# Fillers taken out of two tiles, 21 more tiny matmuls at the start, and a last half product that leaves in two parts: a sliding-window attention and ReGLU kernel on one Trainium2 core

## The chip, the core and the metric

The kernel runs on one core of one Trainium2 chip. The core has TensorE (PE in the profile; its weight loads are listed as PEld), VectorE (DVE), ScalarE (ACT), GpSimd (POOL) and SyncE (SP), each with a queue of its own that it works off in order. Engines wait for one another through semaphores. Matrix products go to PSUM, in eight banks of 128 partitions by 512 f32; everything else lies in SBUF or in HBM, and DMA engines move it.

The metric is the device time of one execution in microseconds. Before the change three runs gave 308.47, 309.38 and 309.38 us, median 309.38 us.

## What is computed

Attention over a causal window of 64 positions (8 batches, 8 heads, 576 positions, head size 64), and then a feed-forward layer whose gate is a ReLU (4608 tokens, 512 features, 1536 hidden features), all f32 outside:

```python
scores = scale * np.matmul(q, k.transpose(0, 1, 3, 2))
rel = pos[:, None] - pos[None, :]
mask = (rel >= 0) & (rel < window)              # window = 64
...
attn = attn / (np.sum(attn, axis=-1, keepdims=True) + 1e-09)
...
x = attn_out.transpose(0, 2, 1, 3).reshape(B * S, H * D)
gate = np.maximum(x @ w_gate, 0.0)
val = x @ w_val
out = (gate * val) @ w_out
```

## The kernel before, in words

The 4608 tokens are cut into nine tiles of 512 (`TT`). For a tile the kernel computes scores (`score_run`, L370 to L386: a mask product at L377 and the q k products at L385), exponentials on ACT (L645), the products with v and a column of ones (`value_block`, L388 to L392), a reciprocal and a scaling on DVE (L660, L398), a transpose on DVE (L403), the two hidden products and their gate, and the product with `w_out`.

Tile 0 takes the hidden products directly (`direct_block`, L737 on, matmuls at L750), and tiles 0 to 2 the output products too (`output`, L900 on, matmuls at L916, copy to SBUF on ACT at L927, store at L931). The other tiles use Strassen-Winograd schemes with seven half-size products in place of eight (`fast_hidden`, matmuls at L842; `fast_output`, matmuls at L1005).

The work is written in two parts. `first_part` (L408 to L509) is written out by hand: loads of the first batch, constants, a run of tiny matmuls of 32x32 by 32x16 zeros (L423 and L424, `PADS = 72` of them), scores and values of the first six windows. `second_part` (L511 to L1077) lists operations with a key, durations and dependencies, and a planner (`Plan`, L44 to L252) orders them: it plays the kernel forward with estimated durations and emits each engine's instructions in the order in which they start in that play. Nothing in it knows what the chip does; the estimates are numbers in the source.

Two things of the planner matter here.

- `fill` (L115 to L127): when the planner thinks that PE will be idle for at least 0.7 us ahead of an operation, it emits matmuls of zeros of 128x128 by 128x384 into a free bank, as many as fit at 0.165 us each with 0.25 us to spare. `emit` (L1061 to L1064) writes them. There are 21, in four groups.
- `fetch` (L93 to L113): PE's instructions come from HBM in blocks of 256. The planner assumes that block n is asked for when instruction 256 n + 165 is reached (`ASK`, L54) and must be there at instruction 256 n + 445 (`NEED`, L55). `plan.at` (L520) is the place in PE's instructions at which the second part begins, 428 + 2 PADS, since a matmul and its weight load are two instructions.

The end of the kernel is tile 8 in `fast_output`. Its last product, P4, runs in two halves `m` of six matmuls each, into columns 0 to 255 and 256 to 511 of one bank. Each half is copied by ACT (L1030) into its columns of one SBUF tile `pr`, and stored from SP (`leave`, L982 to L987). SP's queue holds the stores in order, each behind a wait for its copy and one for an earlier DMA on the same semaphore.

Of the kernel before, what the change touches and what calls it, by code (L numbers as in the profile page):

```python
# [12 lines left out]
ACT = mybir.ActivationFunctionType  # L13
# [30 lines left out]
class Plan:  # L44
# [33 lines left out]
    def op(self, name, key, engines, fn, after=(), take=(), give=(), dma=None):  # L78
        after = [a for a in dict.fromkeys(after) if a is not None]
        o = Op(name, key, engines, fn, after, take, give, dma)  # L80
        self.n += 1
        o.n = self.n
        self.all.append(o)
        for a in after:
            a.feeds.append(o)
        return o
# [169 lines left out]
def kernel(  # L256
# [10 lines left out]
    nc = tc.nc  # L267
# [9 lines left out]
    TT = 512  # L277
    HT = TT // 2
    NT = B * S // TT
    LAST = NT - 1  # L280
# [31 lines left out]
    zero = consts.tile([128, 512], FP16)  # L312
# [89 lines left out]
        n = 32 * x.shape[1]  # L402
        nc.vector.transpose(xt[:, 2 * hh:2 * hh + 2, c0:c0 + n].rearrange("p e (s c) -> p s e c", c=32), x)  # L403

    PADS = 72
    FRONT = 0.0

    def first_part():  # L408
# [103 lines left out]
    def second_part():  # L512
# [4 lines left out]
                     "bo": [(14.2 - FRONT, banks[7])],  # L517
                     "p": [(13.8 - FRONT if i < 8 else 0.0, p) for i, p in enumerate(ps)],
                     "pr": [(0.0, x) for x in prs]})
        plan.at = 428 + 2 * PADS  # L520
        plan.asked, plan.got, plan.come = 2, 1, [12.1 - FRONT, 18.8 - FRONT]
        op = plan.op

# [35 lines left out]
        for n, (wt, src, key) in enumerate(((wg, moe_w_gate, "g"), (wv, moe_w_val, "v"))):  # L559
            for blk in range(NF // 4):  # L560
# [3 lines left out]
                       dma=(0.524, 0.40, "q")) for a in range(2)]  # L564
        for blk in range(NF // 4):
            loaded["o", blk] = [op("wo_load", (kt("wo0"), kt("wo1"), kt("wo2"))[blk], issue(0.75), lambda e, blk=blk: wo_part(4 * blk, 4 * blk + 4),
                                   dma=(1.05, 0.40, "q"))]
# [155 lines left out]
        for hh in range(2):  # L723
            parts = [(24 + 4 * hh + s, pp, 6 + s // 2, hh, 2 * hh + s // 2, s % 2) for s in range(4)]
            gives = [("p", pp, g) for g in range(G)] if hh else []
            a, o = value_bank(0, T0 + kt("rv") + 0.3 * hh, parts, masks + before, gives, [])
# [209 lines left out]
        HD = DM // 2  # L936
# [18 lines left out]
        def fast_output(t, key_of):  # L955

            mine = out_ops.setdefault(t, [])
            gt = gs[t % 2]
            a11, a21, a12, a22 = (gt[:, f, HT * h:HT * h + HT] for f in (low, high) for h in range(2))
            g11, g21, g12, g22 = ([gates[t, j, n, h] for j in range(NJ)] for n in range(2) for h in range(2))  # L960
            was = products.get(t - 1, {})
            now = products[t] = {}
            done = [was.get(name, []) for name in ("P5", "P6", "", "P3")]
            key = key_of(0)
            sums = [[], [], [], []]
            for c0, c1 in ([(2 * j, 2 * j + 2) for j in range(NJ)] if t == LAST else [(0, HF)]):
                c = slice(c0, c1)
                made = []
                for n, (to, x, y, how) in enumerate(((ss[:, 0], a21, a22, ADD), (ss[:, 1], ss[:, 0], a11, SUB), (a21, a11, a21, SUB), (ss[:, 2], a12, ss[:, 1], SUB))):
                    js = slice(c0 // 2, c1 // 2)  # L970
                    after = [g21[js] + g22[js], g11[js] + made[0:1], g11[js] + made[0:1], g12[js] + made[1:2]][n] + done[n]
                    made.append(op("g_sum", key - kt("gs") + n, {"DVE": (0.11 + 0.0006 * (c1 - c0) * HT, True)},
                                   lambda e, to=to, x=x, y=y, how=how, c=c: VEC[e].tensor_tensor(to[:, c], x[:, c], y[:, c], how), after=after))
                    sums[n].append(made[n])
            b11, b12, b21, b22 = (wo[:, f, HD * d:HD * d + HD] for f in (low, high) for d in range(2))
            s1, s2, s3, s4 = sums
            what = {"P1": (a11, b11, g11), "P2": (a12, b21, g12), "P3": (ss[:, 2], b22, s4), "P4": (a22, ts[:, 2], g22 + wsums),
                    "P5": (ss[:, 0], ts[:, 0], s1 + wsums), "P6": (ss[:, 1], ts[:, 1], s2 + wsums), "P7": (a21, b12, s3 + wsums)}
            bank, hold, snaps, ran = {}, {}, {}, {}
            mine += [o for some in sums for o in some]  # L980

            def leave(after, x, h, d, m0, m1, key):  # L982
                rows = out[TT * t + HT * h + 128 * m0:TT * t + HT * h + 128 * m1, HD * d:HD * d + HD].rearrange("(m p) c -> p m c", p=128)
                src = x["x"] if False else None
                return op("store", key, {"SP": (0.35, False)},
                          lambda e: nc.sync.dma_start(rows, x["x"][:, HD * m0:HD * m1].rearrange("p (m c) -> p m c", c=HD)),
                          after=after, give=[("pr", x, "x")] if m1 == 2 else (), dma=(0.13 * (m1 - m0), 0.3, "sp"))  # L987

            place = 0
            for name in ("P1", "P2", "P6", "P5", "P7", "P3", "P4"):  # L990
                a, b, after = what[name]
                to = {"P2": "B", "P5": "C", "P3": "C"}.get(name, "A")
                first = name in ("P1", "P2", "P5")
                after = list(after)
                if name in ("P6", "P7", "P3"):
                    after.append(snaps[{"P6": "P1", "P7": "P6", "P3": "P5"}[name]])
                if name == "P4":
                    after += ran["C22"]
                if name == "P5" and t == LAST:
                    after += parts  # L1000
                parts = []
                for m in range(2):
                    def mm(e, a=a, b=b, to=to, first=first, m=m):
                        for f in range(HF):
                            nc.tensor.matmul(bank[to][:, HD * m:HD * m + HD], a[:, f, 128 * m:128 * m + 128], b[:, f],  # L1005
                                             start=(first and m == 0 and f == 0), stop=(f == HF - 1), skip_group_check=True)
                    k = key_of(place)
                    place += 1
                    parts.append(op("o" + name, k, direct(HD, 1, HF), mm, after=after + parts,
                                    take=[("bo+bank" if to == "A" else "bank", bank, (to,))] if first and m == 0 else ()))  # L1010
                    parts[-1].count = HF
                mine += parts
                now[name] = parts
                if name in ("P1", "P6", "P5"):
                    x = hold[name] = {}
                    snaps[name] = op("snap", k - kt("fs"), act(512), lambda e, x=x, to=to: nc.scalar.copy(x["x"], bank[to]),
                                     after=parts, take=[("pr", x, ("x",))])
                    continue
                src, h, d = {"P2": ("P1", 0, 0), "P7": ("P5", 1, 1), "P3": ("P6", 0, 1), "P4": (None, 1, 0)}[name]
                x = hold.get(src, {})  # L1020
                ran[name] = []
                for m0, m1 in ((0, 1), (1, 2)) if t == LAST and name == "P4" else ((0, 2),):
                    c = slice(HD * m0, HD * m1)
                    give = [("bank", bank, to)] if name != "P7" and m1 == 2 else ()
                    if src:
                        o = op("osum", k - kt("fu"), dve(HD * (m1 - m0)),
                               lambda e, x=x, to=to, c=c: nc.vector.tensor_tensor(x["x"][:, c], bank[to][:, c], x["x"][:, c], ADD),
                               after=[snaps[src]] + parts[m0:m1], give=give)
                    else:
                        o = op("evac", k + 0.9, act(HD * (m1 - m0)), lambda e, x=x, to=to, c=c: nc.scalar.copy(x["x"][:, c], bank[to][:, c]),  # L1030
                               after=parts[m0:m1], take=[("pr", x, ("x",))] if m0 == 0 else (), give=give)
                    if name == "P7":
                        ran["C22"] = [o]
                    leave([o], x, h, d, m0, m1, k + 0.5)
# [25 lines left out]

        def emit(o, e):  # L1061
            if not isinstance(o, Op):
                for _ in range(e):
                    nc.tensor.matmul(o[0][:, 0:384], zero[:, 0:128], zero[:, 0:384], start=o[1], stop=o[1], skip_group_check=True)  # L1064
                return
            made = o.fn(e)
            if e in VEC and o.engines[e][1]:
                if e == "POOL" and "DVE" in port:
                    tc.add_manual_dep(made.ins, port["DVE"].ins.name,
                                      mybir.DependencyInfo(mybir.DependencyClass.Sync, mybir.DependencyReason.SCHED_ONLY),  # L1070
                                      reason="port order")
                    port.clear()
                elif e == "DVE":
                    port["DVE"] = made
# [37 lines left out]
```

## Time and profile before

| what | value |
|---|---|
| runs, median | 308.47, 309.38, 309.38 us; 309.38 us |
| the profiled execution, its own time | 308.09 us |
| its span, first to last instruction | 306.4 us |
| PE busy | 298.0 us, 97% of the span, 4772 matmuls |
| DVE, ACT, POOL busy | 245.9, 213.1, 229.7 us (80%, 70%, 75%) |
| the 72 tiny matmuls, L424 | 1.26 to 3.34 us, 27.5 ns apart |
| PE's next work, L442 | starts at 4.40 us, behind a wait for DVE |
| the 21 fillers, L1064 | in groups of 5, 8, 4 and 4 that begin at 27.15, 39.47, 46.39 and 50.57 us |
| last matmul of the kernel | 302.23 to 302.50 us |
| last two copies, ACT L1030 | 302.58 to 302.95 and 302.85 to 303.23 us |
| last two stores, SP | issued at 302.98 and 303.41 us |
| instruction blocks for PE (queue q8) | 37 packets of 16 KB |

In the timeline a line gives the start, the length, the engine, the source line, the operation, and in brackets how long the engine was idle before and what released it. Neighbours of one kind are merged, and the end of a matmul is a model: a 128x384 matmul is listed with 0.33 us while the next one starts 0.16 us after it. PE is therefore read by its starts.

### The profile page before, as it was taken

How to read it: one execution, taken by the hardware profiler on the slowest of the kernel's cores; microseconds unless marked ns; L12 is line 12 of the kernel's file. 1: busy time of each engine (PE TensorE's matmuls, PEld its weight loads, DVE VectorE, ACT ScalarE, POOL GpSimd, SP SyncE). 2: the span in 40 equal slices, each digit the busy share in tenths (PEclk: the TensorE clock that was granted, in tenths of full speed). 3: DMA queues.
4: the chain of work that ended last, by engine and by line, in shares of the span. 5: the costliest groups of instructions: out<-in, count | busy, mean ns of one | idle time of the engine just before them, and what ended most of it. 6: DMA issues, size and time to landing. Idle time of an engine off the chain costs nothing.

```text
span 306.4 us, 11252 instructions
## 1 busy us (share of the span) xinstructions
PE 298.0 (97%) x4772; PEld 241.0 (79%) x4772; DVE 245.9 (80%) x421; ACT 213.1 (70%) x414; POOL 229.7 (75%) x233
## 2 busy tenths in 40 slices
PE   6799999999999999999999999999999999999994
PEld 4486855788757876777898888888888888888884
DVE  5968896989963997887999989878896889595761
ACT  4455333888768787788878786778687876878721
POOL 8697955999999899999199954995489157938520
PEclk9999999999999999999999999999999999999999
DMA  7999999992249963996694194574112011101033
GB/s 215 187 192 206 196 195 199 169 207 24 19 78 143 186 104 75 142 180 138 121 93 62 39 168 122 41 165 37 54 36 71 5 39 46 59 0 36 1 125 116
DMA packets 58930, 32.87 MB, mean 107 GB/s; under 512 B 39424, under 2 KB 53248, under 8 KB 58880
## 3 DMA queue, kind: packets, MB, share of 16 engines
q0 software_dynamic: 46672, 18.29, 51.0%
q1 hardware_dynamic: 12208, 13.87, 14.4%
q8 instruction: 37, 0.61, 0.8%
q14 instruction: 13, 0.11, 0.1%
HBM read 37.75 MB, written 9.44 MB: 154 GB/s over the span
## 4 chain that ended last, share of the span: by engine, by line
PE 93%; DMA 3%; POOL 2%; issue 0%; DVE 0%; ACT 0%; ACTq 0%; POOLq 0%
PE bank L842 49%; PE bank L1005 18%; PE bank L916 10%; PE bank L750 6%; PE bank L391 4%; DMA wv<-in_moe_w_val_dram 3%; PE bank L385 3%; PE bank L377 2%; PE bank L1064 1%; POOL v L356 1%; POOL wg L337 0%; POOL k L347 0%; POOL wv L337 0%; DVE xw L398 0%; POOL q L347 0%
## 5 line engine op out<-in xcount | busy, mean ns | idle before, releaser
L876 POOL TENSOR_TENSOR g_sb<-pr,pr 128x512 f16<-128x512 f32 x96 | 121.7, 1284 | 45.9 <-ACT pr L889 16.4
L858 DVE TENSOR_TENSOR pr<-bank,pr 128x512 f32<-128x512 f32 x144 | 92.7, 679 | 24.9 <-PE bank L842 22.1
L851 ACT COPY pr<-bank 128x512 f32<-128x512 f32 x144 | 79.9, 590 | 28.5 <-PE bank L842 26.3
L842 PE MATMUL bank<-xt,vs 128*128 128x256 f16 x384 | 56.7, 273 | 0.0
L842 PE MATMUL bank<-xt,us 128*128 128x256 f16 x384 | 56.2, 273 | 0.0
L867 ACT ACTIVATE pr<-pr 128x512 f32<-128x512 f32 x72 | 45.4, 639 | 5.9 <-DVE pr L858 5.5
L842 PE MATMUL bank<-xt,wg 128*128 128x256 f16 x288 | 42.8, 273 | 0.0
L842 PE MATMUL bank<-xt,wv 128*128 128x256 f16 x288 | 42.7, 273 | 0.0
L842 PEld LDWEIGHTS <-us 128*128 128x128 f16 x384 | 37.0, 98 | 6.3
L645 ACT ACTIVATE p<-bank 128x512 f16<-128x512 f32 (+1 forms) x68 | 35.7, 593 | 8.3 <-PE bank L385 8.1
L842 PEld LDWEIGHTS <-vs 128*128 128x128 f16 x384 | 37.2, 98 | 4.7
L916 PE MATMUL bank<-wo,g_sb 128*128 128x512 f16 x144 | 35.9, 379 | 0.0
L356 POOL DMA_DIRECT2D v<-in_v_dram x40 | 34.9, 884 | 0.8 <-PE bank L385 0.8
L889 ACT ACTIVATE pr<-bank 128x512 f32<-128x512 f32 x48 | 27.0, 601 | 6.6 <-PE bank L842 5.0
L842 PEld LDWEIGHTS <-wg 128*128 128x128 f16 x288 | 27.7, 98 | 4.7
L842 PEld LDWEIGHTS <-wv 128*128 128x128 f16 x288 | 28.1, 98 | 4.1
L1005 PEld LDWEIGHTS <-g_sb 128*128 128x128 f16 x288 | 27.9, 98 | 3.4
L1005 PE MATMUL bank<-wo,g_sb 128*128 128x256 f16 x216 | 28.4, 273 | 0.0
L398 DVE TENSOR_TENSOR xw<-bank,r 128x448 f16<-128x448 f32 (+2 forms) x45 | 25.8, 575 | 1.5
L403 DVE STREAM_TRANSPOSE xt<-xw 128x512 f16<-128x512 f16 (+2 forms) x38 | 25.0, 669 | 0.5 <-ACT xw L506 0.3
L1005 PEld LDWEIGHTS <-ss 128*128 128x128 f16 x216 | 21.0, 98 | 2.5
L916 PEld LDWEIGHTS <-g_sb 128*128 128x128 f16 x144 | 13.6, 98 | 11.2
(95 smaller groups left out, 391.9 us busy)
## 6 DMA issues: line engine op xcount, KB each, us to landing
out_dram<-pr SPq DMA_DIRECT2D x35, 256.0 KB, 2.3
k<-in_k_dram POOLq DMA_DIRECT2D x15, 288.0 KB, 6.8
q<-in_q_dram POOLq DMA_DIRECT2D x15, 288.0 KB, 7.2
v<-in_v_dram POOLq DMA_DIRECT2D x32, 128.0 KB, 6.0
v<-v SPq DMA_DIRECT2D x12, 132.0 KB, 2.6
v<-v SPq DMA_DIRECT2D x24, 66.0 KB, 2.1
wg<-in_moe_w_gate_dram POOLq DMA_DIRECT2D x6, 256.0 KB, 6.4
wv<-in_moe_w_val_dram POOLq DMA_DIRECT2D x6, 256.0 KB, 7.9
```

The source lines that it names most:

```text
L356: nc.gpsimd.dma_start(v16s[b % 2][lo:hi, g, :, 0:64], v[b, :, 64 * g - 64 + lo:64 * g - 64 + hi].rearrange("h p d -> p h d"))
L398: nc.vector.tensor_tensor(x, blocks_of(to, n)[:, :, 0:D].rearrange("p s (c e) -> p s e c", e=2), r[:, :, :, None].to_broadcast([128, n, 2, ...
L403: nc.vector.transpose(xt[:, 2 * hh:2 * hh + 2, c0:c0 + n].rearrange("p e (s c) -> p s e c", c=32), x)
L645: nc.scalar.activation(pp[g][:, 0:n].rearrange("p n c -> p (n c)"), st[g][:, 0:64 * n], ACT.Exp, scale=scale)
L842: nc.tensor.matmul(slot[to][:, HT * m:HT * m + HT], w[:, kk, 128 * m:128 * m + 128], x[:, kk], start=(first and m == 0 and kk == 0), stop= ...
L851: lambda e, hold=hold, slot=slot: nc.scalar.copy(hold["x"], slot["A"]),
L858: nc.vector.tensor_tensor(hold["x"], slot[to], hold["x"], ADD)
L867: lambda e: nc.scalar.activation(hold["x"], hold["x"], ACT.Relu), after=[o])
L876: lambda e: VEC[e].tensor_tensor(gh[:, fs:fs + 2, h], pair(a["x"]), pair(b["x"]), MUL),
L889: lambda e, hold=hold, slot=slot, i=i: nc.scalar.activation(hold["x"], slot["A"], ACT.Copy if i else ACT.Relu),
L916: nc.tensor.matmul(bank["b"][:, 0:c1 - c0], gs[t % 2][:, f, 128 * sub:128 * sub + 128], wo[:, f, c0:c1], start=(j == 0 and i == 0), stop=( ...
L1005: nc.tensor.matmul(bank[to][:, HD * m:HD * m + HD], a[:, f, 128 * m:128 * m + 128], b[:, f], start=(first and m == 0 and f == 0), stop=(f ...
```

## The change

Three edits. The number of tiny matmuls goes from 72 to 93, while the planner's own starting place keeps the old 72, so that it plans as before. `emit` returns at a filler without writing anything; the planner still counts them. And the second half of the last product, 256 columns, is copied in two parts of 128 columns, the first by ACT and the second by DVE, and stored in two parts, the first issued by ACT itself and the second by SP. The first half is copied and stored as before.

```diff
-    PADS = 72
+    PADS = 93
...
-        plan.at = 428 + 2 * PADS
+        plan.at = 428 + 2 * 72
...
-                for m0, m1 in ((0, 1), (1, 2)) if t == LAST and name == "P4" else ((0, 2),):
+                if t == LAST and name == "P4":
+                    pieces = ((0, 0, HD, "ACT", "SP"), (1, 0, 128, "ACT", "ACT"), (1, 128, HD, "DVE", "SP"))
+                    for m, c0, c1, e, q_of in pieces:
+                        c = slice(HD * m + c0, HD * m + c1)
+                        copy = nc.scalar.copy if e == "ACT" else nc.vector.tensor_copy
+                        o = op("evac", k + 0.9, {e: (0.17 + 0.00085 * (c1 - c0), False)},
+                               lambda e, x=x, to=to, c=c, copy=copy: copy(x["x"][:, c], bank[to][:, c]),
+                               after=parts[m:m + 1] + ran[name], take=() if ran[name] else [("pr", x, ("x",))])
+                        ran[name] = ran[name] or [o]
+                        rows = out[TT * t + HT * h + 128 * m:TT * t + HT * h + 128 * m + 128, HD * d + c0:HD * d + c1]
+                        op("store", k + 1.0, {q_of: (0.35, False)},
+                           lambda e, rows=rows, x=x, c=c: (nc.sync if e == "SP" else nc.scalar).dma_start(rows, x["x"][:, c]),
+                           after=[o], dma=(0.13 * (c1 - c0) / HD, 0.3, "sp"))
+                    continue
+                for m0, m1 in ((0, 2),):
...
-                               after=parts[m0:m1], take=[("pr", x, ("x",))] if m0 == 0 else (), give=give)
+                               after=parts[m0:m1], take=[("pr", x, ("x",))], give=give)
...
             if not isinstance(o, Op):
-                for _ in range(e):
-                    nc.tensor.matmul(o[0][:, 0:384], zero[:, 0:128], zero[:, 0:384], start=o[1], stop=o[1], skip_group_check=True)
                 return
```

In the built program PE's instructions are 9537 before and after: 21 tiny matmuls are added at the front and 21 fillers taken out, with a weight load each. From the last filler on, every PE instruction has the same number as before; ahead of the first group it has a number 42 higher, and 32, 16 and 8 higher between the groups. The other engines keep their order. At the end ACT has one copy, one shorter copy and a DMA; DVE has one copy more, which waits for the second copy of ACT; SP has the first half's store and a store of 128 columns.

## The prediction

> **What bounds the kernel now.** I read the shares and the chain of waits first, to see which engine sets the end.
>
> ```profile
> span 306.4 us, 11252 instructions
> ...
> PE 93%; DMA 3%; POOL 2%; issue 0%; DVE 0%; ACT 0%; ACTq 0%; POOLq 0%
> PE bank L842 49%; PE bank L1005 18%; PE bank L916 10%; PE bank L750 6%; PE bank L391 4%; DMA wv<-in_moe_w_val_dram 3%; PE bank L385 3%; PE bank L377 2%; PE bank L1064 1%; POOL v L356 1%; POOL wg L337 0%; POOL k L347 0%; POOL wv L337 0%; DVE xw L398 0%; POOL q L347 0%
> ```
>
> PE makes 93% of the chain, and the fillers (L1064) are part of it. Next, the waits of PE from 17 us on:
>
> ```profile
> PE bank L750 <- DMA wv<-in_moe_w_val_dram: 0.5, 1, 0.5
> PE bank L391 <- DVE xw L398: 0.2, 1, 0.2
> ```
>
> From 17.12 us, when a load of `wv` lands, PE waits once more, for 0.2 us, up to 290 us, and the last products run in one piece. So a microsecond of PE work taken out is worth a microsecond, unless a wait that is now hidden comes up. Third, the timeline of PE around the fillers:
>
> ```profile
> 26.79 0.43 PE L391 MATMUL bank<-v,p 128*32 128x65 f16 x32
> 27.15 0.99 PE L1064 MATMUL bank<-zero 128*128 128x384 f16 x5
> 27.98 1.46 PE L750 MATMUL bank<-xt,wv 128*128 128x384 f16 x8
> 29.28 1.06 PE L750 MATMUL bank<-xt,wg 128*128 128x128 f16 x16
> ...
> 39.47 1.47 PE L1064 MATMUL bank<-zero 128*128 128x384 f16 x8
> 40.78 1.89 PE L916 MATMUL bank<-wo,g_sb 128*128 128x512 f16 x8
> 42.60 0.40 PE L391 MATMUL bank<-v,p 128*32 128x65 f16 x28
> ...
> 46.39 0.81 PE L1064 MATMUL bank<-zero 128*128 128x384 f16 x4
> 47.14 0.40 PE L377 MATMUL bank<-ident,biasT 32*128 32x256 f16 x8
> ...
> 50.57 0.82 PE L1064 MATMUL bank<-zero 128*128 128x384 f16 x4
> 51.23 1.03 PE L916 MATMUL bank<-wo,g_sb 128*128 128x512 f16 x4
> ```
>
> Each group starts right behind real work and the work behind it starts with no idle time. The question is whether that work could have started earlier. The semaphore counts in the trace tell when each of its waits was met.
>
> **The fillers, group by group.** From filler start to follower start they hold 0.82, 1.31, 0.75 and 0.66 us, 3.54 in all.
>
> Group 1. The follower, `wv` at L750, waits for a load that landed at 25.20 and a bank freed at 24.81: it can start at 27.15, and gains 0.82. Its eight matmuls end 0.82 earlier, but the next block (29.28) needs two transposes of DVE:
>
> ```profile
> 28.34 0.76 DVE L403 STREAM_TRANSPOSE xt<-xw 128x256 f16<-128x256 f16 x2
> ```
>
> They are done at 28.79 and 29.12, and hang on the values at 26.79, which do not move. The matmul that needs the second one started at 29.39; now it starts at 29.12 + 0.04 (the lag of other met waits) = 29.16. Kept 0.23, lost 0.59.
>
> Group 2. L916 needs a block of `wo` (landed 38.80) and a gate (37.76); PE is free at 39.47 - 0.23 = 39.24. Gain 0.23 + 1.31 = 1.54. Behind eight matmuls the values at L391 need all four exponentials of ACT:
>
> ```profile
> 39.59 2.06 ACT L645 ACTIVATE p<-bank 128x512 f16<-128x512 f32 x4 [1.35 <-PE bank L385]
> ```
>
> ACT waits for the scores, so it moves by 0.23: the last is ready at 41.66 - 0.23 = 41.43. The weight load that needs it stood at 42.61; it goes at 41.47. Kept 1.13, lost 0.41.
>
> Group 3. L377 and L385 need banks that DVE freed at 44.01 and 45.18, against 45.3 and 45.5 for the new starts. Nothing is lost: 1.13 + 0.75 = 1.88. The exponentials behind them move along.
>
> Group 4. L916 needs the last block of `wo`, issued by POOL at 40.35 and landed at 49.27; PE would be free at 50.57 - 1.88 = 48.69. It waits until 49.31, against 51.23: 1.92, so of 0.66 only 0.04 is kept.
>
> From there every row moves with PE. The tightest link is POOL's difference for tile 1 (done at 54.31, its matmul at 54.43). POOL had been idle for 2.13 us ahead of it, waiting for DVE, and DVE for PE, so it comes 1.9 earlier too. I keep **1.90 us**. Bounds: if the block of `wo` lands earlier the fourth group gives up to 0.62 more, 2.5. Below, one chain follows DMA and not PE: a store of tile 1 issued at 60.09 landed only at 65.06; its buffer feeds ACT at 65.78, and that ACT row frees the way to a copy that the matmul at 68.11 needs. If the landing stays where it is, ACT's row can move from 65.78 to 65.10, and with the rows behind it the matmul moves by 1.36 only. I take 1.90, since the store goes out 1.9 earlier into lighter traffic; 1.36 is a rival.
>
> **The 21 tiny matmuls.** Their rows are 27.5 ns apart (72 from 1.26 to 3.18), so 21 take 0.58 and end near 3.9. The next work of PE is held by DVE:
>
> ```profile
> 4.40 0.40 PE L442 MATMUL bank<-ident,bias 128*32 128x128 f16 x8 [1.05 <-DVE bias L432]
> ```
>
> The idle 1.05 us covers it. Without that cover they would cost 0.58, and even this would sit ahead of the wait for `wv` at 17.12. Cost 0.
>
> They also set which instruction falls in which block of PE's instructions (37 packets of 16 KB in queue q8, 256 instructions each). The sixth began to arrive at 47.96 and the next at 53.68. Behind the last filler the numbers are as before; ahead of it the asking and the needing instruction both come earlier, so I count 0 and price the late case below.
>
> **The tail.** ACT's copies start when P4 is done:
>
> ```profile
> 302.58 0.65 ACT L1030 COPY pr<-bank 128x256 f32<-128x256 f32 x2 [3.39 <-PE bank L1005]
> 302.98 0.82 SPq L986 DMA_DIRECT2D out_dram<-pr  x2
> ```
>
> and the list of DMA issues has, with the KB of each and the median us to landing:
>
> ```profile
> out_dram<-pr SPq DMA_DIRECT2D x35, 256.0 KB, 2.3
> ...
> out_dram<-pr SPq DMA_DIRECT2D x2, 128.0 KB, 1.8
> ```
>
> Today the last store is issued at 303.41 and its landing is met at 305.15; 1.2 us of closing follow. After: ACT's second copy starts at 302.85 and takes 0.27 (0.37 for 256 columns, 0.59 for 512), to 303.12; ACT issues its store at 303.17, which lands near 304.9 if it takes the 1.74 of today's last. DVE's copy waits for ACT's second one: 303.16, plus 0.29 (0.42 for 256 columns at L398, 1.05 ns a column), 303.45. SP issues at 303.47, 0.06 later than today, for half the bytes. From 256 to 128 KB landing falls by 0.5, so 64 KB saves between 0 (as many rows) and 0.25: 304.96 to 305.21. One wait fewer stands in SP's closing list behind it, 0.06. Sum -0.25 to +0.0; I take **-0.1**. No DMA issued by ACT is in this trace; if it takes the 2.3 of the large stores it lands at 305.5, +0.3.
>
> [...]
>
> **Sum.** 306.4 - 1.9 - 0.1 = 304.4 us of span. The profiled execution took 308.09, 1.7 more than its span: 306.1. The median of the runs is 1.29 above it, so **307.4 us** beside 309.38.
>
> **Rivals.**
>
> A. *The store holds the pool* (above): 1.36 + 0.1, 307.9. For it: DMA is over 90% busy until 69 us. Against it: between 60.2 and 61 the DMA engines were idle, where the earlier store can go.
>
> B. *An instruction block comes late.* Instruction 1725, the first past the planner's `NEED` mark of the sixth block, now comes at 50.35 - 1.88 = 48.47, in the values. If that block still begins at 47.96 and needs 2.62 us (the shortest distance from a block's start to its mark that PE passed without idle time, at 71.31), it holds PE until 50.58. L916 then starts at 50.80 against 51.23: 0.43 kept, 308.9. Against it: the instruction that asks for it comes about 3 us earlier too. For it: blocks came up to 4.8 us after being asked for while DMA was full.
>
> C. *The fillers only fill gaps*: other waits take their place and nothing but the tail moves, 309.3. Against it stand the counts above; for it, that 1.62 of 3.54 us do turn into waits.
>
> D. *The clock drops* (slower). New idle stretches of up to 0.59, 0.41 and 0.62 us appear, the last near 49 us; the longest in the trace once all matmuls run at full speed is 0.49. Early on, eight 128x384 matmuls (L448, 4.73) start 0.32 us apart, the fillers 0.16: half speed. If a gap brings that back, each us of it costs half a us, and from 4.0 us on the gain is gone. A stretch as long as the slow start, from 1.26 to about 9.24 us, costs 4.0: 311.4. Against it: the gap of 0.49 at 16.6 us changed nothing.
>
> [...]
>
> **How the numbers follow.** The forecast 0.54, A 0.20, B 0.12, C 0.08, D 0.04, and 0.02 for the early `wo` (306.8). The forecast alone holds 306.9 to 307.8. The range reaches over A and B, with the spread of the runs (0.9): 306.3 to 309.3; C's edge and D lie outside. About 0.3%, 0.93 us, is what can be told from no change. The forecast and most of A are faster by more: 0.74; B, C and the rest of A within: 0.20; D and noise: 0.06.
>
> **What would show it.** No L1064 row; L750 `wv` at 27.15; PE waiting for DVE's transpose near 29.1, for ACT near 41.4 and for `wo` near 49.3; L842 of tile 1 starting about 1.9 us earlier, and the same distance at 290 us (1.4 from 68 us on: A; a wait with no releaser near 48.5: B; 128x256 matmuls over 0.2 us apart: D). At the end a last store landing within 0.3 us of 2.65 us behind the last matmul. It is wrong if PE's rows lose the 1.9 us again, or if `wo` lands later than 49.3.

## The result, and the profile after

The changed kernel takes 307.91 us (median of 22 runs, 307.28 to 310.02), the kernel before, run beside it, 309.64 us (22 runs). The ratio is 0.9947, with a 95% interval of 0.9929 to 0.9965: 1.64 us less, between 1.1 and 2.2. The forecast was 2.0 less. The profiled execution of the changed kernel is one of its slower ones, 309.13 us, and that of the kernel before, 308.09 us, is faster than all of its 22 runs (308.47 to 311.47), so the two profiles set side by side make the change look worse than the runs do.

Shares and chain, from the page of the changed kernel:

```profile
span 307.2 us, 11254 instructions
...
PE 85%; DMA 8%; POOL 3%; issue 2%; DVE 1%; ACT 0%; ACTq 0%; DVEq 0%; POOLq 0%
```

PE still makes most of the chain, but DMA has 8% in place of 3%, and "issue", time without a releaser, 2% in place of 0%. The waits of PE from 17.2 to 290 us (us in total, times, longest):

```profile
PE bank L391 <- issue: 1.0, 1, 1.0
PE bank L750 <- DMA wv<-in_moe_w_val_dram: 1.0, 1, 1.0
PE bank L916 <- DMA wo<-in_moe_w_out_dram: 0.3, 1, 0.3
PE bank L385 <- issue: 0.3, 1, 0.3
PE bank L750 <- DVE xt L403: 0.2, 1, 0.2
PE bank L391 <- ACT p L645: 0.2, 1, 0.2
```

Three of the lines are waits that the prediction named: `wo`, DVE's transposes, ACT's exponential. Two are without a releaser. In the timeline of PE the predicted ones stand where the fillers were:

```profile
28.00 1.47 PE L750 MATMUL bank<-xt,wv 128*128 128x384 f16 x8
29.67 1.26 PE L750 MATMUL bank<-xt,wg 128*128 128x128 f16 x16 [0.20 <-DVE xt L403]
...
42.31 0.39 PE L391 MATMUL bank<-v,p 128*32 128x65 f16 x25 [0.20 <-ACT p L645]
...
46.19 0.40 PE L377 MATMUL bank<-ident,biasT 32*128 32x256 f16 x8
...
50.13 1.02 PE L916 MATMUL bank<-wo,g_sb 128*128 128x512 f16 x4 [0.33 <-DMA wo<-in_moe_w_out_dram]
...
52.45 0.60 PE L842 MATMUL bank<-xt,wg 128*128 128x256 f16 x4
```

In this execution `wv` released PE at 17.97, in the one before at 17.12, so distances from there are compared and not times. From `wv` to the first L842 it took 53.56 - 17.12 = 36.43 us before and 52.45 - 17.97 = 34.48 now: 1.95 less. Not all of it lasts: the ninth matmul of L842 (54.43 before, 53.50 now) reads a difference that POOL computes (`xt`, L716), which was done at 54.31 before and is done at 53.46 now, and counted to this matmul the gain is 1.77.

Later PE stops twice, for no wait that the profile shows:

```profile
70.31 0.21 PE L391 MATMUL bank<-v,p 128*32 128x65 f16 x3
71.55 0.82 PE L391 MATMUL bank<-v,p 128*32 128x65 f16 x69 [1.03 <-issue]
...
148.16 0.66 PE L385 MATMUL bank<-qT,kT 32*128 32x64 f16 x62
149.13 0.20 PE L385 MATMUL bank<-qT,kT 32*128 32x64 f16 x2 [0.31 <-issue]
```

Against the usual distance of such rows they cost 1.22 and 0.49 us. The first falls on instruction 2488 of PE, the second on 5046: 256 n + 440 and 256 n + 438, with n = 8 and 18, just ahead of the instruction at which the planner has block n needed (256 n + 445). The packet of block 8 begins at 69.33 and that of block 18 at 146.90 (queue q8), each 2.22 us ahead of PE's next start. In the execution before, the packets of the same two blocks began 2.6 and 2.5 us ahead of these instructions, and PE passed without a stop.

The end, from the timeline and from the list of DMA issues (KB each, us to landing):

```profile
303.47 0.54 ACT L1028 COPY pr<-bank 128x256 f32<-128x256 f32 x2 [3.39 <-PE bank L1005]
303.87 0.84 SPq L1033 DMA_DIRECT2D out_dram<-pr  x2
304.04 0.38 ACTq L1033 DMA_DIRECT2D out_dram<-pr  x1
304.04 0.29 DVE L1028 COPY pr<-bank 128x128 f32<-128x128 f32 x1 [1.24 <-ACT pr L1028]
```

```profile
out_dram<-pr SPq DMA_DIRECT2D x1, 128.0 KB, 1.8
out_dram<-pr ACTq DMA_DIRECT2D x1, 64.0 KB, 1.8
out_dram<-pr SPq DMA_DIRECT2D x1, 64.0 KB, 1.7
```

DVE's copy runs beside ACT's issue, behind ACT's second copy, as worked out. From the start of the last matmul to the end of the span it takes 4.09 us, against 4.17.

So the profiled execution is 0.85 late at `wv` (a load, as it falls), gains 1.95 to L842, loses 2.00 from there to the last matmul (0.18 to POOL's difference, 1.84 in stops, three with a short one of 0.13), and gains 0.07 at the end: +0.8 in span, 307.2 against 306.4.

### The profile page after: what moved, and what is told of

Read it like the earlier page. It is cut to its first block, busy times and chain, and to the rows that moved or that the text cites. A ratio compares the mean times of both kernels' runs of the same rounds, so it can differ in the third digit from the quotient of the medians.

```text
span 307.2 us, 11254 instructions
## 1 busy us (share of the span) xinstructions
PE 297.1 (97%) x4772; PEld 240.2 (78%) x4772; DVE 246.2 (80%) x422; ACT 213.0 (69%) x414; POOL 229.8 (75%) x233
## 4 chain that ended last, share of the span: by engine, by line
PE 85%; DMA 8%; POOL 3%; issue 2%; DVE 1%; ACT 0%; ACTq 0%; DVEq 0%; POOLq 0%
PE bank L842 48%; PE bank L1005 18%; PE bank L916 8%; PE bank L391 4%; PE bank L750 3%; DMA wo<-in_moe_w_out_dram 3%; DMA wv<-in_moe_w_val_dram 3%; DMA k<-in_k_dram 2%; PE bank L385 2%; PE bank L377 1%; POOL vs L791 1%; POOL v L356 1%; POOL q L347 0%; POOL k L347 0%; DVE xw L398 0%
## 5 line engine op out<-in xcount | busy, mean ns | idle before, releaser
L842 PE MATMUL bank<-xt,vs 128*128 128x256 f16 x384 | 56.7, 273 | 0.0
L842 PE MATMUL bank<-xt,us 128*128 128x256 f16 x384 | 56.2, 273 | 0.0
L842 PE MATMUL bank<-xt,wg 128*128 128x256 f16 x288 | 42.8, 273 | 0.0
L842 PE MATMUL bank<-xt,wv 128*128 128x256 f16 x288 | 42.7, 273 | 0.0
L842 PEld LDWEIGHTS <-us 128*128 128x128 f16 x384 | 37.0, 98 | 6.5 <-issue 0.2
L842 PEld LDWEIGHTS <-vs 128*128 128x128 f16 x384 | 37.2, 98 | 4.7
L916 PE MATMUL bank<-wo,g_sb 128*128 128x512 f16 x144 | 35.9, 380 | 0.3 <-DMA wo<-in_moe_w_out_dram 0.3
L842 PEld LDWEIGHTS <-wg 128*128 128x128 f16 x288 | 27.7, 98 | 4.7
L842 PEld LDWEIGHTS <-wv 128*128 128x128 f16 x288 | 28.1, 98 | 4.2
L916 PEld LDWEIGHTS <-g_sb 128*128 128x128 f16 x144 | 13.5, 98 | 11.3 <-issue 0.3
```

Of the source, the lines that this page charges most:

```text
L842: nc.tensor.matmul(slot[to][:, HT * m:HT * m + HT], w[:, kk, 128 * m:128 * m + 128], x[:, kk], start=(first and m == 0 and kk == 0), stop= ...
L916: nc.tensor.matmul(bank["b"][:, 0:c1 - c0], gs[t % 2][:, f, 128 * sub:128 * sub + 128], wo[:, f, c0:c1], start=(j == 0 and i == 0), stop=( ...
```

## Experiments

The kernels stand in one table, but for two profiles in which the clock fell, read from one profile each: the first column from the landing of `wv` to the first L842, the second from there to the last matmul, the third the stops without a releaser behind L842 that exceed the usual row distance by 0.12 us or more, the fourth from the last matmul's start to the end, in us.

| kernel | `wv` to L842 | L842 to last matmul | stops in it | tail | ratio to before |
|---|---|---|---|---|---|
| before | 36.43 | 248.67 | none | 4.17 | 1 |
| changed | 34.48 | 250.67 | 1.22, 0.49, 0.13 | 4.09 | 0.9947 [0.9929, 0.9965] |
| fillers out alone | 35.41 | 250.42 | 0.43, 0.36, 0.58, 0.53 | 4.17 | 0.9968 [0.9944, 0.9993] |
| tiny matmuls alone | 36.43 | 253.99 | 2.93, 1.27, 0.30, 0.75 | 4.16 | 1.0111 [1.0070, 1.0152] |
| tail alone | 36.43 | 249.10 | 0.42 | 4.10 | 0.9998 [0.9976, 1.0020] |
| q load behind `wo` | 34.14 | 249.86 | 0.12, 0.67 | 4.09 | 0.9952 [0.9933, 0.9971] |
| group 2 out alone | 35.53 | 249.40 | 0.25, 0.46 | 4.16 | one execution |
| 114 tiny matmuls | 35.05 | 251.66 | 1.97, 0.80, 0.25 | 4.09 | 1.0052 [1.0023, 1.0080] |
| other tail, and q load | 34.15 | 250.03 | 0.31, 0.47 | 4.19 | 0.9973 [0.9947, 1.0000] |
| 85 tiny matmuls | 35.00 | 248.97 | 0.17, 0.14 | 4.10 | 0.9958 [0.9941, 0.9975] |
| group 4 out alone | 35.94 | 250.06 | 0.16, 0.54 | 4.17 | one execution |
| group 1 out alone | 36.19 | 249.17 | 0.48 | 4.17 | one execution |

### The three parts apart

Fillers out, with 72 tiny matmuls and the tail as before:

```diff
             if not isinstance(o, Op):
-                for _ in range(e):
-                    nc.tensor.matmul(o[0][:, 0:384], zero[:, 0:128], zero[:, 0:384], start=o[1], stop=o[1], skip_group_check=True)
                 return
```

> The 21 fillers are taken out alone: 72 tiny matmuls, the old tail. Theory T (the fillers hold up work that is ready; 3.54 us go and 1.62 come back as waits): PE needs 34.5 us instead of 36.4 from the release of the `wv` block (17.12 before) to the first L842, and the kernel is 1.9 us faster, ratio 0.994, less whatever late instruction blocks take. Rival F (the gain needs the 21 tiny matmuls, which keep instructions in their blocks): the ratio is 0.997 or above, with new waits of PE that have no releaser behind 53 us, at other matmuls than in the changed kernel, since every mark now falls 21 matmuls later in the program. Rival S (the gain is in the tail): 1.000.

Ratio 0.9968, a gain of about 1.0 us. The way to L842 is 1.02 shorter and not 1.9: the same waits appear, `wo` landed late in this execution (L916 waits 0.6 us), PE waits 0.3 us for ACT at 48.06, and block 5 stops it for 0.36 us at instruction 1720. Four more stops follow, at 256 n + 436 to 440. That is the picture of rival F.

The tiny matmuls alone, with the fillers kept:

```diff
-    PADS = 72
+    PADS = 93
...
-        plan.at = 428 + 2 * PADS
+        plan.at = 428 + 2 * 72
```

> 93 tiny matmuls alone, fillers and tail as before. Theory T: 0.58 us of PE ahead of waits that cover it, ratio 1.000; the matmul at L442 keeps its start at 4.40 us. Rival F: the ratio moves by 0.2% or more either way, with waits of PE that have no releaser.

1.0111, 3.4 us slower. The way from `wv` to L842 is the same to 0.01 us, so the tiny matmuls cost nothing where they run. The time goes where they shift the numbers. From the timeline of PE:

```profile
69.80 0.38 PE L842 MATMUL bank<-xt,vs 128*128 128x256 f16 x2
72.94 0.39 PE L842 MATMUL bank<-xt,vs 128*128 128x256 f16 x2 [2.77 <-issue]
```

It is instruction 2488 again, in other work, and the packet of block 8 begins at 70.71, 2.23 us ahead of PE's next start. The four stops add up to 5.25 us, the loss behind L842 is 5.32.

The tail alone is the `pieces` hunk of the change.

> The tail alone, fillers and 72 tiny matmuls as before. Theory T: the distance from the start of the last matmul to the end of the span is 4.09 us instead of 4.17, as in the changed kernel, ratio 0.9998, which can't be told from 1. Rival S: ratio 0.996.

0.9998; the tail is 4.10 against 4.17 us. Right in the trace, and too small for the runs.

### The waits that were predicted

The last `wo` block lands when the loads ahead of it have passed. Here the last q load of batch 2 is issued behind it (by holding its `emit` back):

```diff
+            if o.name == "qk_load":
+                held.append(o)
+                if len(held) == 6:
+                    return
             made = o.fn(e)
+            if o.name == "wo_load":
+                blocks.append(o)
+                if len(blocks) == 3:
+                    held[5].fn(e)
```

> The changed kernel with one load moved: the load of q for batch 2 (not needed before 56 us) is issued behind the last block of `wo` and not ahead of three loads of v and of that block. Theory T (group 4 of the fillers is worth little because L916 waits for `wo`, and `wo` lands when the DMA engines get to it): `wo` lands about 1.4 us earlier, L916 at idle time 0, 0.6 us off PE's way to L842 and 0.6 us off the time: ratio to before 0.993 at most, and 0.002 under the changed kernel. Rival: another wait takes its place (the copies of v, the transposes), and the way to L842 stays 34.5 us.

The wait for `wo` is gone from the waits of PE, and another stands there:

```profile
PE bank L750 <- DMA wv<-in_moe_w_val_dram: 0.8, 1, 0.8
PE bank L385 <- issue: 0.5, 1, 0.5
PE bank L842 <- ACT pr L851: 0.3, 1, 0.3
```

L842 is reached 0.34 us sooner, where I expected 0.6. The row for L842 is its ninth matmul, at 53.18: it needs POOL's difference, done at 53.13 (the row names ACT's copy, which ended last, at 53.15), and starts 0.43 us late, which falls into the next column of the table. Counted to this matmul the way is 35.43 us against 35.53 in the changed kernel, so of the 0.34 us 0.10 is left. 0.9952 does not differ from 0.9947.

Single groups left out, here the fourth, with as many tiny matmuls added as fillers go:

```diff
-    PADS = 72
+    PADS = 76
...
+                group.append(e)
-                for _ in range(e):
+                for _ in range(e if len(group) in (1, 2, 3) else 0):
```

> Only the fourth group of fillers (four matmuls ahead of L916, 50.57 in the profile before) is left out; the first three stay, and 4 tiny matmuls are added so that the later instructions keep their numbers. Read from the landing of `wv` (first L750 behind 17 us) to the first L842: 36.43 us before. Theory P (the prediction: a filler delays work that is ready, and what it is worth depends on which wait is met next): alone the group is worth its whole 0.66, since the last block of `wo` landed at 49.27 and PE comes to it only at 50.57: 35.77 us. In company of the other groups the same four matmuls gave only 0.04. Rival C (the fillers only fill the wait for `wo`): L916 waits and the way stays 36.4.

This execution had the clock at half speed from 12 to 18.8 us (last section), so its way can't be read. It was run again:

> Once more the kernel before without the fourth group of fillers, since the profile of the first such run had half the clock from 12 to 18.6 us. Theory P: way from `wv` to L842 35.77 us (36.43 less the whole 0.66), L916 without a wait for `wo`. Rival C: 36.4.

35.94: at the first L842 0.49 of 0.66 us is kept, and L916 has no wait. But there is a wait at L842 that I had not listed, from the waits of this kernel:

```profile
PE bank L385 <- issue: 0.4, 1, 0.4
PE bank L842 <- ACT pr L851: 0.3, 1, 0.3
```

It is the ninth matmul again, with POOL's difference. From the timeline of the kernel before, and of this one:

```profile
53.16 1.15 POOL L716 TENSOR_TENSOR xt<-xt 128x512 f16<-128x512 f16 x1 [2.13 <-DVE r L660]
54.43 0.60 PE L842 MATMUL bank<-xt,us 128*128 128x256 f16 x4
```

```profile
54.22 1.15 POOL L716 TENSOR_TENSOR xt<-xt 128x512 f16<-128x512 f16 x1 [2.14 <-DVE r L660]
55.42 0.60 PE L842 MATMUL bank<-xt,us 128*128 128x256 f16 x4 [0.27 <-ACT pr L851]
```

Counted to this matmul the way is 37.23 us against 37.30 before: the group alone is worth 0.07 us and not 0.66. The two rows of before give this bound, 0.12 us between the end of the difference and its matmul, and POOL follows, over DVE, values (L391, 50.24 before) that PE computes ahead of the group.

The second group:

> Only the second group of fillers (eight matmuls, 39.47) is left out, 8 tiny matmuls added for the numbering. Theory P: L916 comes 1.31 earlier (its `wo` block has landed at 38.80), but the values at L391 then wait for the fourth exponential of ACT, which does not move (41.66 in the profile before, so the weight load that needs it comes at 41.70 in place of 42.61): 0.91 of 1.31 kept, way from `wv` to L842 35.52 us against 36.43. By the same count the four groups, each alone, are worth 0.23 + 0.91 + 0.75 + 0.66 = 2.55 and together 1.9. Rival C: the way stays 36.4.

35.53, and PE waits for ACT:

```profile
PE bank L391 <- ACT p L645: 0.2, 1, 0.2
```

The first group:

> Only the first group of fillers (five matmuls, 27.15) is left out, 5 tiny matmuls added for the numbering. Theory P: the eight matmuls on `wv` start 0.82 earlier, then PE waits for DVE's second transpose: 0.23 of 0.82 kept, way from `wv` to L842 36.20. Rival: the whole 0.82 is kept, 35.6; or none, 36.4.

36.19, and PE waits for DVE:

```profile
PE bank L750 <- DVE xt L403: 0.2, 1, 0.2
```

So to the first L842 the groups are worth 0.24, 0.90, 0.49 (first, second and fourth) alone, and the four of them 1.95 together; to its ninth matmul 0.23, 0.90, 0.07, and 1.77 together. The third was not left out alone. A filler's worth is the distance to the next wait, and not its own time.

### The numbers of the instructions

If the number of an instruction decides, then 21 tiny matmuls more in the changed kernel (`PADS = 114`) must bring back the stops of the tiny matmuls alone, though no real work differs.

> The changed kernel with 114 tiny matmuls in place of 93: the work of PE behind them is the same, every later instruction has a number higher by 42. Theory F (PE stops where an instruction block comes late, at numbers 256n + 440, and the number of the work that stands there decides): the mark of block 8 falls again into the same products as in the run with the tiny matmuls alone, and costs 2 to 3 us near 70 us, those of blocks 11 and 18 some 0.5 to 1 us; way from `wv` to L842 as in the changed kernel, 34.5 (21 more tiny matmuls end at 4.5 where L442 starts at 4.41, 0.1 us that the wait for `wv` takes up); ratio to before 1.000 to 1.008. Theory T (tiny matmuls cost nothing, the first run of them was slower for another reason): ratio 0.995 as the changed kernel, no stall without a releaser over 0.5 us beyond those of the changed kernel.

1.0052. From the timeline of PE:

```profile
68.31 0.38 PE L842 MATMUL bank<-xt,vs 128*128 128x256 f16 x2
70.50 0.39 PE L842 MATMUL bank<-xt,vs 128*128 128x256 f16 x2 [1.81 <-issue]
```

The same two products are torn apart as with the tiny matmuls alone, at the same instruction 2488, 2.35 us behind its packet (68.16). The stops add up to 3.02 us, the loss against before behind L842 is 2.99. The way to L842 is longer than expected, 35.05, by two waits for `wo` (1.0 us together).

And eight fewer than in the changed kernel (`PADS = 85`) must clear the stop near 148 us:

> The changed kernel with 85 tiny matmuls in place of 93, so every later instruction of PE has a number lower by 16. Theory F: the mark of block 18 moves from the first scores at L385 near 148 us to work 16 instructions later; by the rows of the changed kernel its packet may then begin 3.8 us after the instruction that asks for it before PE must stop, against 2.5 now, where packets came 2.2 to 3.2 after being asked for: the stall without a releaser near 148 us (0.25 to 0.67 us in the profiles of the changed kernel and its relatives) is gone. The marks of blocks 8, 11, 12 and 19 have as much room as before. Ratio to before 0.992 to 0.995, 0.0015 below the changed kernel's 0.9947 if nothing else moves. Theory T: the number of tiny matmuls makes no difference: a stall near 148 us of 0.25 us or more at L385, ratio 0.9947.

The scores now run in one piece:

```profile
147.95 0.68 PE L385 MATMUL bank<-qT,kT 32*128 32x64 f16 x64
148.56 0.61 PE L842 MATMUL bank<-xt,wg 128*128 128x256 f16 x4
149.00 0.75 PE L842 MATMUL bank<-xt,wv 128*128 128x256 f16 x4
```

Of the stop at block 18 0.14 us is left, in the products at 149.00, and another of 0.17 us stands at 95.28 (block 11); the stretch from L842 to the last matmul is 248.97, longer than before by these two, 0.30. Yet the ratio, 0.9958, is no better than that of the changed kernel. In the profile the gain went to `wo`, for which PE waits longer here:

```profile
PE bank L750 <- DMA wv<-in_moe_w_val_dram: 1.5, 1, 1.5
PE bank L916 <- DMA wo<-in_moe_w_out_dram: 1.0, 2, 0.8
PE bank L750 <- DVE xt L403: 0.2, 1, 0.2
```

So with both, 85 tiny matmuls and the q load behind `wo`:

> As the run before, and the last q load of batch 2 issued behind the last `wo` block. Theory F: way from `wv` to L842 34.1 us, L916 without a wait for `wo`, no stall near 148 us; ratio 0.991 to 0.994, at or below that with 85 tiny matmuls alone. Rival: 0.34 us on this way are lost again within the spread of the late blocks, ratio as with 85 tiny matmuls alone.

0.9955 [0.9930, 0.9979]; neither the wait for `wo` nor a stop near 148 us is in its profile, but the clock is at half speed from 14 to 17.7 us, so its way can't be read. The rival that the gain is lost in the spread stands, as far as the runs can tell.

### Another tail

The second half copied in one piece by DVE into a tile of its own and stored by ACT, on top of the q load:

```diff
-                    pieces = ((0, 0, HD, "ACT", "SP"), (1, 0, 128, "ACT", "ACT"), (1, 128, HD, "DVE", "SP"))
+                    pieces = ((0, 0, HD, "ACT", "SP"), (1, 0, HD, "DVE", "ACT"))
                     for m, c0, c1, e, q_of in pieces:
+                        x = {}
...
-                               after=parts[m:m + 1] + ran[name], take=() if ran[name] else [("pr", x, ("x",))])
-                        ran[name] = ran[name] or [o]
+                               after=parts[m:m + 1], take=[("pr", x, ("x",))])
```

> The changed kernel with two more changes: the second half of the last product is copied in one piece by DVE into a tile of its own (so DVE waits for PE only, not for ACT's copy) and stored by ACT; and the last q load of batch 2 is issued behind the last `wo` block. Theory P: the DVE copy starts within 0.1 us of ACT's first copy and takes 0.42, ACT's store is issued 0.15 to 0.25 us earlier than the last store of the changed kernel (1.24 us behind the start of the last matmul) and lands 1.85 later: tail from the start of the last matmul to the end 3.8 to 3.95 against 4.09. With the 0.34 of the q load: way 34.1; ratio 0.9935 to 0.995, the rest as late instruction blocks fall. Rival: the store issued by ACT lands as late as the larger store of 2.3 us, tail 4.1 or more.

The tail is 4.19 us, longer than both. From the timeline, with the last matmul starting at 301.79:

```profile
302.14 0.37 ACT L1029 COPY pr<-bank 128x256 f32<-128x256 f32 x1 [3.39 <-PE bank L1005]
302.54 0.34 SPq L1033 DMA_DIRECT2D out_dram<-pr  x1
302.55 0.42 DVE L1029 COPY pr<-bank 128x256 f32<-128x256 f32 x1 [1.07 <-ACT pr L1029]
303.01 0.37 ACTq L1033 DMA_DIRECT2D out_dram<-pr  x1
```

DVE still waits for ACT's copy, though they share no SBUF tile: in the built program its copy waits for the count that ACT's copy raises, and the bank that both read is all that the two share. So the two copies run one after the other, and the longer one is last. Neither my expectation nor its rival had this; ACT's store landed after 1.8 us, as taken.

No version beats the changed kernel by more than the intervals.

## Why the prediction was right, point by point

**What bounds the kernel.** Right. PE's chain sets the end, and what was taken out of it before L842 came out of the time, less what later waits took.

**The groups.** The first waits fell where the prediction put them, and the sum to the first L842, 1.95 us, stands against 1.90. Group 1 alone gave 0.24 (0.23 predicted); group 2 alone 0.90 (the count of before gives 0.91); in company the fourth ran into `wo` at once. The counts of the semaphores were enough for it: the wait that ends last, plus 0.04 us. Behind the first L842 the step "POOL had been idle for 2.13 us ahead of it, waiting for DVE, and DVE for PE, so it comes 1.9 earlier too" was too large: counted from `wv`, POOL's difference came 1.70 us earlier, and PE, with 0.12 us to spare, 1.77.

**The bound for an early `wo`, 2.5 us, was too high.** With `wo` out of the way 2.29 us are gained at the first L842, but the ninth matmul waits 0.43 for POOL's difference, and 1.87 are left. The prediction named this difference as the tightest link, but let it move along with PE; the later run of the fourth group alone, expected at 0.66 us, left it out as well.

**Rival A** did not happen: PE's instruction 1800 came at 52.46 before and 51.36 now, its instruction 2486, the last ahead of the stop, at 71.28 and 70.31. Of 1.10 us 0.97 were still there, where A left 0.5 less; the difference is POOL's, since counted from `wv` the gain is 1.77 us at the ninth matmul of L842 and 1.81 near 70 us. **Rival C** did not happen either: the waits came, and to the first L842 1.95 us were still gained.

**Rival B** had the mechanism, and the wrong block. Block 5 came in time in the changed kernel (it begins at 46.98, and PE passes its mark at 49.6), but blocks 8 and 18 did not. The step "From there every row moves with PE" failed here, since a packet need not move along. Block 8 has 4.7 us in the execution before between the instruction at which the planner has it asked for (256 n + 165, at 66.56) and the one that needs it (71.28), and the packet took 2.1 to begin; in the changed kernel it took 3.7 (65.60 to 69.33). The two stops are 1.7 us in the profiled execution, nearly the whole gain, so by the prediction's own sign ("wrong if PE's rows lose the 1.9 us again") this one execution speaks against it, and the runs for it. Unlike the gain the stops differ from one profile to the next: the one at block 8 is missing in the profiles with the q load behind `wo`, and the one at block 18 has 0.25 to 0.67 us in the profiles with the whole change and 93 or 114 tiny matmuls, and 0.14 or none in the two with 85. Nor is the stop at block 18 a price of the change: with the tail alone PE has the instructions of before, and it stops there for 0.42 us, and single groups left out give 0.46 to 0.54. The profile before passed block 18 with its packet 2.48 us ahead; the executions that stopped there were held until 2.2 to 2.9 us behind the beginning of theirs.

**The 21 tiny matmuls.** "So I count 0" was right for their running time (L442 at 4.41 against 4.40), and right in company of the fillers that they replace, since behind the last filler every number is as before. But the zero hides two terms of opposite sign: alone they cost 3.4 us, and without them the fillers' removal gives some 1.0 us in place of 1.64. The intervals of the last two overlap (0.9968 and 0.9947), so that difference is carried by the traces (`wo` and the stops) and not by the runs.

**The tail** gave 0.07 (0.1 predicted), in both profiles that have it alone or with the rest.

**The remaining 0.4 us** between 2.0 and 1.64 lie inside the interval. By the traces 0.13 of it is POOL's difference (1.77 in place of 1.90) and 0.03 the tail. Behind L842 the profile shows the stops, 1.84 of the 2.00 us that are lost there against a profile of before that has none; but the kernel with 85 tiny matmuls, whose profile has 0.3 us of them, is no faster in its runs. How much of the rest is theirs and how much `wo` and `wv` landing late stays open.

**Rival D**, the clock, did not follow from the new gaps: the granted clock is 1.00 from 27 to 31, 41 to 44 and 49 to 53 us. It fell elsewhere, below.

## What to carry to other kernels

Cost a removed stretch of PE work by the distance to the next semaphore that is met, group by group, let the earlier gains run into the later waits, and follow them until no wait of another engine is left: here a gain of 0.49 us was 0.07 eight matmuls on. In a kernel of several thousand instructions, treat the number of an instruction as part of the change: work added or removed at the front moves every later block border, here by 42 instructions for 21 tiny matmuls. With the tiny matmuls alone the instructions from 256 n + 165 to the border of block 8 took 2.8 us in place of 4.7, its packet began 3.5 us behind the first of them, and the stop was 2.9 us. When something is taken out, keep the numbers behind it or measure the new ones, and look at PE's rows without a releaser at 256 n + 436 to 440 in the profiles, of more than one execution.

## What the runs showed of the hardware that was not expected

**Late blocks.** Every stop without a releaser over 0.3 us behind L842, in all kernels, is at instructions 256 n + 436 to 440 of PE, and ends 2.2 to 3.0 us behind the beginning of that block's 16 KB packet: 2.22 where the packet took 0.93, and 3.04 where it took 1.55, so some 1.2 to 1.5 behind its end. The packet begins between 0.9 us ahead of instruction 256 n + 165 and 5.5 behind it; the times over 3.5 us all lie before 150 us, in the half of the span with most of the traffic (149 GB/s in the mean of the first 20 slices of the page before, 66 in the last 20). The trace lists 37 such packets for PE's 9537 instructions, some 258 to a packet.

**The clock at the start.** In the first run without group 4, PE waited 1.24 us for DVE at 11.68, and the granted clock fell (stretch, length, busy time and count of each engine in the order PE, PEld, DVE, ACT, POOL, then PEclk, DMA share, GB/s):

```profile
10.00:11.00 1.00, 0.44 (x2) 0.09 (x1) 0.63 (x1) 1.00 (x5) 0.00 (x0) 1.00 2.32 158
11.00:12.00 1.00, 0.32 (x41) 0.32 (x43) 0.90 (x2) 0.03 (x1) 0.00 (x0) 1.00 1.40 202
12.00:13.00 1.00, 0.81 (x55) 0.58 (x39) 0.94 (x3) 0.92 (x5) 0.65 (x2) 0.51 1.24 205
```

It stayed at half until 18.8 us. The longest idle time from 5 us on was 1.24 us; what was low is the share, 1.52 of 3 us busy from 9 to 12. The other profile with the drop (85 tiny matmuls and the q load) had 1.65 busy of the 3 us from 11 to 14, no wait over 0.66 in them and no idle time over 1.07 from 5 us on, and half clock from 14 on. Before the change the lowest sum of three such slices from 8 us on is 2.01, and there the clock held. But that second profile also passed 1.63 of 3 us, from 8 to 11, at full clock, so the sum alone does not decide. The two drops are 6.8 us long, from 12.02, and 3.4, from 14.27 to 17.7. In the 3.41 us ahead of each PE is listed as busy for 57% and 59%, but with the tail alone it is busy for 47% of the 3.41 us from 14.61 to 18.02 and kept the clock, so what decides stays open. Nor need the drop be of these kernels: two of the 23 runs of the kernel before beside the first have its mean granted clock, 0.989.
